# Paired butterfly outputs, quartered fifth denominator tiles and a last unit moved behind three stores, in a one-core kernel of memory attention and a spectral filter

## The chip, the core and the metric

The kernel runs on one core of a Trainium2 chip. That core has five engines that run side by side, each through its own queue in order: TensorE (PE, matrix products into PSUM; its weight loads are shown apart as PEld), VectorE (DVE), ScalarE (ACT), GpSimd (POOL) and SyncE (SP, which here issues most transfers between SBUF and DRAM). The metric is the device time of one execution in microseconds (us); less is better. Operands are fp32, or fp32 cut to a shorter mantissa (fp32r), which the kernel uses as a high and a low part.

## What is computed

Two independent parts stand beside each other in the output. Part A is an attention with a compressive memory: 2048 tokens of width 576, 32 heads of 18, four segments of 512 tokens. Part B is a global filter: a two-dimensional real FFT of a 2048 × 576 array, a product with a complex weight, and the inverse FFT.

```python
def _A_ref(x, wq, wk, wv, wo, beta):          # S=2048, H=32, Dh=18, N=4, L=512
    ...
    for s in range(N):
        qs, ks, vs = q[:, :, s], k[:, :, s], v[:, :, s]
        p = _softmax(einsum("bhqd,bhkd->bhqk", qs, ks) * scale + mask)
        a_dot = einsum("bhqk,bhkd->bhqd", p, vs)
        pq = phi(qs)
        num = einsum("bhld,bhde->bhle", pq, M)
        den = einsum("bhld,bhd->bhl", pq, z)[..., None] + 1e-6
        outs.append(g * num / den + (1.0 - g) * a_dot)
        pk = phi(ks)
        M = M + einsum("bhld,bhle->bhde", pk, vs)
        z = z + einsum("bhld->bhd", pk)
    return concat(outs) @ wo
def _B_ref(x, w_r, w_i):
    X = rfft2(x) * (w_r + 1j * w_i)
    return irfft2(X, s=(S, D))
```

## The kernel before

**Stages.** The FFT over the 2048 rows is split as 128 × 4 × 4. The forward part (`FFT.forward`, L108) does the transform over columns and the 128-point one as matmuls, in 20 iterations `u`, and leaves 16 complex blocks in the tile `Z` of 128 partitions × 4 × 4 × 2 × 290: block (b, a), real and imaginary part, 290 frequencies. Then come radix-4 butterflies over a and over b on DVE (`bf`, L199), the twiddle factors between them (`tws`, L210), the weight product and the way back (`middle`, L232; `last`, L270). `FFT.inverse` (L285) brings the blocks back with matmuls. From 72 to 280 us, between the forward and the inverse matmuls, stand the projections of part A (`projections`, L549): for each of four groups g nine q/k units and four v units. Then attention runs over 132 turns (`attention`, L941), and a tail projects the last segment (`last_proj`, L901).

**The FFT's vector work is paced.** `stage1`, `middle` and `last` are generators; each `yield` is one step. `Pace` (L88) holds them in a queue with a hand-written total: 61 steps for the four first-stage generators, 165 for the middle and 40 for the last. The forward transform takes one step per iteration for u < 14 (the first generator is queued at u = 7) and two from u = 14. The projections spread what is left, less 10 for the last butterfly (`tot=pace.left-10`, L558), over their units: `w=tot/(36+16*2.4)` steps for a q/k unit and 2.4 times as many for a v unit, 0.4 of them before and 0.6 after the second half of the unit's products. The order in which each engine sees its work in these stages is the order of the code.

**A q/k unit** (`qk_unit`, L466) makes 14 products of 512 columns (L464) into a PSUM bank, and then splits the result into three bfloat16 parts while later units run on PE: ACT copies it (L477) and, where needed, takes a negative-side exponential (L480, L481); DVE forms the feature map (L483) and subtracts the first part (L484); ACT copies the second part (L491); PE subtracts it (L493, after the first seven products of the unit after next); ACT copies the third (L494).

**A butterfly** (`bf`) has ten steps: four DVE operations over whole blocks (128x580) into temporaries, two whole ones for outputs 0 and 2, and four of half a block (128x290) for the outputs 1 and 3, whose parts are rotated by 90 degrees (L204 to L209). **A twiddle** (`tws`) multiplies a block by exp(i a): ACT makes cos(a) and sin(a) times the whole block (L218, L219), DVE combines halves (L224, L226). Where the angle is 90 degrees (exponent 4), the same work is done.

**Denominators.** For segments 1 to 3 `den` (L781) multiplies the feature maps of the queries by z. The heads lie in five tiles, four of 7 heads (126 rows) and one of 4 heads (72 rows). z stands in `zst`, zero apart from one column per head, 32 columns wide. Tiles 0 to 3 go to the four 32-row column groups of one PSUM bank; tile 4 follows one step later, alone, into a fresh PSUM tile. Each of the two is copied by ACT (L789). Five transfers then write the rows to `dD` in DRAM, and `recip` (L752) reads them back, inverts them and writes them in bfloat16 parts. `den` is one of the background generators `bg` of the attention, which `run_bg` (L953) advances by about 1.2 steps a turn; `later(1, f)` (L907) hands a transfer to the end of the next turn. `post` (L800) gives these products their PSUM bank, of which there is one.

**The tail.** Unit u of `last_proj` is one half row (288 columns) of one of four token blocks; its 15 products run over five tiles t. Before the change the order is: t = 0 to 2 for units 0 to 6, t = 3 for them, t = 0 to 3 for unit 7 (L1041), then t = 4 for all, each followed by a copy out of PSUM on ACT or DVE and, after the second half of a block, a store of 128x576 (L1048). The fifth tile's low part is made on DVE at L893.

## Time and profile before

| | us |
|---|---|
| median of 3 runs (lowest to highest) | 710.68 (708.92 to 712.03) |
| the profiled execution | 709.86 |
| its span, first to last instruction | 708.2 |
| PE busy in the span | 678.8 |
| DVE busy | 544.8 |
| ACT busy | 455.8 |
| GpSimd busy | 194.6 |

One execution is profiled in every instruction. Its span leaves out what lies before the first and after the last instruction. A row of the timeline names start, duration, engine, line, operation, written and read tiles, shape (partitions x elements), the count of equal instructions merged, and in brackets how long the engine had been idle and what released it. A row of the waits view names who waited for whom, the sum, how often, and the longest. Products overlap one another on PE, so what a product costs is the time to the start of the next one, not its own duration. "q" behind an engine's name is its queue: it marks the issue of a transfer.

### The profile page before, as it was taken

The page shows a single profiled execution, that of the slowest core. Times are in us where ns is not written, and L with a number is a line of the kernel's source. Part 1 is how long each engine was busy: PE and PEld are TensorE (multiplying, and loading weights), DVE is VectorE, ACT ScalarE, POOL GpSimd, SP SyncE. Part 2 cuts the span into 40 slices and gives each one's busy share as a digit, 9 for nine tenths or more (in the row PEclk, how much of TensorE's full clock was granted, in tenths as well). Part 3 has the DMA queues.
Part 4 walks back from the last instruction along what each step waited for, and adds up shares of the span by engine and source line. Part 5 has one row for each costly group of instructions (what it writes and reads, how often), then busy time and mean ns, then how long its engine had stood idle before and what let it go on. Part 6 is the DMA issues. An engine that isn't in the chain of part 4 may idle for free.

```text
span 708.2 us, 14408 instructions
## 1 busy us (share of the span) xinstructions
PE 678.8 (96%) x4991; PEld 501.3 (71%) x4991; DVE 544.8 (77%) x1258; ACT 455.8 (64%) x1004; POOL 194.6 (27%) x392
## 2 busy tenths in 40 slices
PE   4999999999999999999999899999999999998997
PEld 3999769879779879998954454445566445663587
DVE  4899969899699789797787787988657876567533
ACT  3777796585686484544388777777656776567421
POOL 3111000100200102665135333444233752235310
PEclk9999999999999999999999999999999999999999
DMA  9897355666384679999338976976766766442151
GB/s 328 256 305 202 115 141 187 186 185 202 100 250 156 178 196 311 202 240 267 100 114 210 190 163 143 207 182 167 154 129 181 182 166 154 92 122 65 29 164 74
DMA packets 71146, 123.80 MB, mean 175 GB/s; under 512 B 12184, under 2 KB 39174, under 8 KB 67482
## 3 DMA queue, kind: packets, MB, share of 16 engines
q1 hardware_dynamic: 64422, 106.89, 57.4%
q0 software_dynamic: 5632, 15.76, 8.2%
q8 instruction: 39, 0.64, 0.4%
q10 hardware_dynamic: 1020, 0.25, 0.2%
q14 instruction: 33, 0.27, 0.1%
HBM read 82.10 MB, written 39.81 MB: 172 GB/s over the span
## 4 chain that ended last, share of the span: by engine, by line
PE 68%; DMA 8%; ACT 4%; DVE 4%; POOL 2%; issue 2%; SPq 0%; ACTq 0%; DVEq 0%; POOLq 0%
PE pj L464 12%; PE pv L734 9%; PE s L656 9%; PE pjv L464 8%; PE po L877 6%; PE i L309 3%; PE i L298 3%; PE s L705 3%; PE s L709 2%; DMA yb<-yout 2%; PE pn L807 2%; PE s L669 2%; PE pm L532 2%; PE s L714 2%; DMA Ks<-qkD 1%
## 5 line engine op out<-in xcount | busy, mean ns | idle before, releaser
L664 DVE CUSTOM_DVE_ANT_0 junk<-s,x 128x512 bf16<-128x512 f32 x248 | 137.0, 552 | 58.0 <-PE s L656 52.6
L719 POOL TENSOR_SCALAR_AFFINE_SELECT P<-P 128x512 f32<-128x512 f32 (+2 forms) x132 | 78.5, 626 | 112.9 <-ACT P L706 104.1
L670 DVE TENSOR_REDUCE mx<-s 128x4 f32<-128x512 f32 x128 | 87.7, 685 | 5.6 <-PE s L669 3.7
L706 ACT ACTIVATE P<-s 128x512 f32<-128x512 f32 x128 | 77.7, 607 | 10.8 <-PE s L705 3.8
L734 PE MATMUL pv<-P,vs 128*32 128x512 f32 (+3 forms) x1024 | 82.5, 439 | 0.1
L715 ACT ACTIVATE P<-s 128x256 f32<-128x256 f32 x128 | 49.8, 389 | 46.1 <-PE s L714 45.7
L711 ACT ACTIVATE P<-s 128x512 f32<-128x512 f32 x128 | 77.4, 605 | 2.4 <-PE s L710 2.2
L656 PE MATMUL s<-Ks,Qs 108*128 108x384 bf16 (+3 forms) x256 | 69.1, 301 | 1.5 <-DMA ux<-uD 1.0
L734 PEld LDWEIGHTS pv<-P,vs 128*32 128x32 f32 x1024 | 26.9, 109 | 45.3 <-issue 35.1
L464 PE MATMUL pj<-x,wqkh 128*128 128x512 f32 x162 | 56.5, 409 | 0.0
L208 DVE TENSOR_TENSOR Z<-t,t 128x290 f32<-128x290 f32 (+1 forms) x96 | 48.4, 553 | 0.1
L656 PEld LDWEIGHTS <-Qs 108*128 108x128 bf16 x320 | 31.5, 98 | 23.5 <-issue 12.1
L208 DVE TENSOR_TENSOR t<-Z 128x580 f32<-128x580 f32 x64 | 46.1, 755 | 0.0
L669 PE MATMUL s<-tri,idb 128*128 128x128 bf16 x256 | 43.0, 219 | 0.0
L522 POOL MEMSET vt<- 128x32 f32 x16 | 2.3, 162 | 141.3 <-PE pm L532 119.5
L298 PE MATMUL i<-civ,Y 128*128 128x256 f32 (+1 forms) x288 | 39.3, 289 | 0.2 <-POOL Y L283 0.2
L298 PEld LDWEIGHTS i<-civ,Y 128*128 128x128 f32 (+1 forms) x288 | 36.5, 181 | 1.0 <-POOL Y L283 0.4
L309 PE MATMUL i<-itab,T 128*128 128x290 f32 (+1 forms) x224 | 36.7, 306 | 0.5 <-DVE yout L317 0.4
L464 PE MATMUL pj<-x,wqkl 128*128 128x512 f32 x90 | 35.6, 395 | 0.0
L464 PE MATMUL pj<-xh,wqkl 128*128 128x512 f32 x90 | 35.5, 395 | 0.0
L143 PE MATMUL f<-ftab,eh 128*128 128x290 f32 x128 | 25.3, 321 | 10.7 <-DMA ftab<-ftab 10.6
L464 PE MATMUL pj<-xh,wqkh 128*128 128x512 f32 x90 | 35.5, 395 | 0.0
(210 smaller groups left out, 1806.3 us busy)
## 6 DMA issues: line engine op xcount, KB each, us to landing
qkD<-sp SPq DMA_DIRECT2D x32, 384.0 KB
xin<-xb SPq DMA_DIRECT2D x16, 384.0 KB
cfw<-cfw POOLq DMA_DIRECT2D x16, 384.0 KB, 4.7
civ<-civ POOLq DMA_DIRECT2D x16, 384.0 KB, 9.0
vs<-vD SPq DMA_DIRECT2D x16, 330.0 KB
vD<-vt SPq DMA_DIRECT2D x16, 311.0 KB
W<-w SPq DMA_DIRECT2D x16, 290.0 KB
yb<-yout SPq DMA_DIRECT2D x16, 290.0 KB
```

Of the source, the lines that this page charges most:

```text
L208: v.tensor_tensor(o,a,b,op=op)
L298: nc.tensor.matmul(p[:m,k],Y[i][:,q,c*128:c*128+m],cc[:,hl,o:o+256],start=n==0,stop=n==5)
L309: nc.tensor.matmul(p,x,t,start=n==0,stop=n==6)
L464: s.nc.tensor.matmul(out,a,b,start=i==0,stop=i==len(L)-1)
L656: nc.tensor.matmul(out,Q[:108,h,128*i:128*i+128],K[:108,h,:128*(i+1)],start=True,stop=True)
L664: nc.vector.tensor_tensor_reduce(out=junk[:,:w],in0=src,in1=s.mask[:,512-w:],scale=1.0,scalar=-3.0e38, op0=OP.add,op1=OP.max,accum_out=s.m ...
L669: nc.tensor.matmul(pa[:,o+w-128:o+w],s.idb,s.tri,start=False,stop=True,skip_group_check=True)
L670: nc.vector.tensor_reduce(out=s.mx[k][:,hh],in_=pa.rearrange("p (b c) -> p b c",c=128),axis=mybir.AxisListType.X,op=OP.max)
L706: nc.scalar.activation(P[0][:,hh],p0,AF.Exp,scale=SC)
L711: nc.scalar.activation(P[1][:,hh],p1,AF.Exp,scale=SC)
L719: nc.gpsimd.affine_select(out=x[:,r],in_=x[:,r],pattern=[[0,r.stop-r.start],[1,128]],compare_op=OP.is_ge,fill=0.0,base=0,channel_multiplie ...
L734: nc.tensor.matmul(s.pvt[32*hh:32*hh+32,128*j:],vt[:,j,19*h:19*h+32],mv[0][:,hh,mv[1]],start=j==0,stop=j>1,skip_group_check=True)
```

## The change

`bf` now works on numbered slots of `Z` (a slot is 290 columns; `slots(i, j)` is a pair of them, j − i apart, which may be negative). The outputs 1 and 3 are made in pairs: one operation writes the real part of one and the imaginary part of the other over 128x580, with the two parts of the fourth temporary read in reverse order. So a butterfly has eight steps. Where output 2 would be turned by 90 degrees afterwards (`turn`), the butterfly writes its two halves turned, in nine steps, and `tws` leaves that block out. `tws` lets ACT make only the cross terms, ±sin(a) times the other half, in two operations of 128x290, and DVE does cos(a) times the block plus the cross terms in one SCALAR_TENSOR_TENSOR of 128x580, in place. The totals of `Pace` become 44, 140 and 32, and 8 steps are kept back for the last butterfly.

z of the fifth tile moves to columns 8 to 11 of its `zst` tile. In `den` its product is cut into four of 128 columns, one for each column group of the bank that holds tiles 0 to 3, accumulated onto it. One ACT copy remains; the fifth tile's rows go out in four transfers of 4 x 128, eight in all, queued one step earlier than the five before.

In the tail the products t = 0 to 3 of unit 7 come after unit 5's copy and the third store; units 6 and 7 are stored separately, 288 columns each.

```diff
@@ -177,7 +177,7 @@
         for i in range(2):
             for x in p: next(x)
         load(3)
-        s.pace=Pace(61+165+40)
+        s.pace=Pace(44+140+32)
         for u in range(20):
             p=prep(u+2) if u+2<16 else iter(())
             if 0<u<17: ev0(u-1)
@@ -196,39 +196,42 @@
             if u>13: s.pace.take(2)
         for _ in wl: pass
         for _ in xs: pass
-    def bf(s,x,y,inv):
+    def slots(s,i,j):
+
+        z=s.Z.rearrange("p b a r f -> p (b a r) f"); d=j-i
+        return z[:,i:j+1:d] if d>0 else z[:,i:j-1 if j>0 else None:d]
+    def bf(s,I,inv,turn=False):
 
         v=s.nc.vector; tp=s.tp
+        x=[s.slots(i,i+1) for i in I]; y=x[2]
         t=[tp.tile([128,2,FP],F32,name=f"t{i}",tag="t",bufs=8) for i in range(4)]
-        p,m=(y[1],y[3]) if not inv else (y[3],y[1])
-        for o,a,b,op in ((t[0],x[0],x[2],OP.add),(t[1],x[0],x[2],OP.subtract),(t[2],x[1],x[3],OP.add),(t[3],x[1],x[3],OP.subtract),
-                         (y[0],t[0],t[2],OP.add),(y[2],t[0],t[2],OP.subtract),
-                         (p[:,0],t[1][:,0],t[3][:,1],OP.add),(p[:,1],t[1][:,1],t[3][:,0],OP.subtract),
-                         (m[:,0],t[1][:,0],t[3][:,1],OP.subtract),(m[:,1],t[1][:,1],t[3][:,0],OP.add)):
+        p,m=(I[3],I[1]) if inv else (I[1],I[3])
+        L=[(t[0],x[0],x[2],OP.add),(t[1],x[0],x[2],OP.subtract),(t[2],x[1],x[3],OP.add),(t[3],x[1],x[3],OP.subtract),(x[0],t[0],t[2],OP.add)]
+        if turn:
+            g,h=(t[2],t[0]) if inv else (t[0],t[2])
+            L+=[(y[:,0],g[:,1],h[:,1],OP.subtract),(y[:,1],h[:,0],g[:,0],OP.subtract)]
+        else: L+=[(y,t[0],t[2],OP.subtract)]
+        L+=[(s.slots(p,m+1),t[1],t[3][:,::-1],OP.add),(s.slots(m,p+1),t[1],t[3][:,::-1],OP.subtract)]
+        for o,a,b,op in L:
             v.tensor_tensor(o,a,b,op=op)
             yield
     def tws(s,L,inv):
 
-        nc=s.nc; v=nc.vector; A=[]; L=[x for x in L if x[1]]
-        if not L: return
-        for i in range(len(L)+1):
-            if i<len(L):
-                y,e=L[i]; a=-2*np.pi*e/16*(-1 if inv else 1)
-                t=[s.tp.tile([128,2,FP],F32,name=f"tw{k}",tag="t",bufs=8) for k in range(2)]
-                nc.scalar.activation(t[0],y,AF.Copy,scale=float(np.cos(a)))
-                nc.scalar.activation(t[1],y,AF.Copy,scale=float(np.sin(a)))
-                A.append((y,t))
-                if i==0: yield
-            if i>0:
-                y,t=A.pop(0)
-                v.tensor_tensor(y[:,0],t[0][:,0],t[1][:,1],op=OP.subtract)
-                yield
-                v.tensor_tensor(y[:,1],t[0][:,1],t[1][:,0],op=OP.add)
-                yield
+        nc=s.nc; q=[]
+        for i,e in L+[(None,0)]:
+            if i is not None:
+                a=-2*np.pi*e/16*(-1 if inv else 1); y=s.slots(i,i+1)
+                t=s.tp.tile([128,2,FP],F32,name="tw",tag="t",bufs=8)
+                for k in range(2): nc.scalar.activation(t[:,k],y[:,1-k],AF.Copy,scale=float((-np.sin(a),np.sin(a))[k]))
+            if q:
+                z,c,x=q.pop(0)
+                nc.vector.scalar_tensor_tensor(z,z,c,x,op0=OP.mult,op1=OP.add)
+            if i is not None: q.append((y,float(np.cos(a)),t))
+            yield
     def stage1(s,b):
-        x=[s.Z[:,b,a] for a in range(4)]
-        yield from s.bf(x,x,False)
-        yield from s.tws([(x[c],b*c) for c in (2,1,3)],False)
+        I=[8*b+2*a for a in range(4)]
+        yield from s.bf(I,False,b==2)
+        if b: yield from s.tws([(I[c],b*c) for c in (2,1,3) if b*c!=4],False)
     def middle(s,wp):
         nc,io=s.nc,s.io; v=nc.vector
         Ws=[]
@@ -238,8 +241,8 @@
             Ws.append(W)
         for i in range(3): ld(i)
         for c in range(4):
-            x=[s.Z[:,b,c] for b in range(4)]
-            yield from s.bf(x,x,False)
+            I=[8*b+2*c for b in range(4)]; x=[s.slots(i,i+1) for i in I]
+            yield from s.bf(I,False)
             for d in range(4):
                 W=Ws[4*c+d]
                 t=s.tp.tile([128,2,FP],F32,name="wm",tag="t",bufs=8)
@@ -253,8 +256,8 @@
                 yield
                 v.tensor_tensor(x[d][:,1],t[:,1],t2[:,0],op=OP.add)
                 yield
-            yield from s.bf(x,x,True)
-            yield from s.tws([(x[b],b*c) for b in (2,1,3)],True)
+            yield from s.bf(I,True,c==2)
+            if c: yield from s.tws([(I[b],b*c) for b in (2,1,3) if b*c!=4],True)
     def inv_setup(s,cp):
         nc,io=s.nc,s.io
         s.cp=cp; s.civ={}
@@ -270,8 +273,7 @@
     def last(s):
 
         for b in range(4):
-            x=[s.Z[:,b,c] for c in range(4)]
-            yield from s.bf(x,x,True)
+            yield from s.bf([8*b+2*c for c in range(4)],True)
             s.done=b
     def ysplit(s,u,eng=None):
         nc=s.nc; eng=eng or nc.gpsimd; b,a=divmod(u,4); x=s.Z[:,b,a]
@@ -539,13 +541,14 @@
             m=tp.tile([126,7,19],F32,name="mm")
             nc.vector.tensor_tensor(m[:r,:w],s.pm[t//3][:r,t%3,:w],s.bm[:r,:w],op=OP.mult)
             M=s.Mst[n][:r,t,:r].rearrange("p (h c) -> p h c",c=18)
-            z=s.zst[n][:r,t,:w]
+            zc=slice(0,w) if t<4 else slice(8,12)
+            z=s.zst[n][:r,t,zc]
             if n==1:
                 nc.gpsimd.tensor_copy(M,m[:r,:w,:18])
                 nc.gpsimd.tensor_copy(z,m[:r,:w,18])
             else:
                 nc.gpsimd.tensor_tensor(M,m[:r,:w,:18],s.Mst[g][:r,t,:r].rearrange("p (h c) -> p h c",c=18),op=OP.add)
-                nc.gpsimd.tensor_tensor(z,m[:r,:w,18],s.zst[g][:r,t,:w],op=OP.add)
+                nc.gpsimd.tensor_tensor(z,m[:r,:w,18],s.zst[g][:r,t,zc],op=OP.add)
     def projections(s,xp,tp,pp,wv,pace,hook):
 
         live=[]
@@ -555,7 +558,7 @@
             for l in list(live):
                 try: next(l)
                 except StopIteration: live.remove(l)
-        tot=pace.left-10
+        tot=pace.left-8
         for g in range(4):
             if g<3: xq=[s.xprep(g+1,t,(xp,s.x0)[g%2],xp,[128,512],"xst",2) for t in range(5)]
             for i in range(13):
@@ -780,17 +783,19 @@
         s.pq[g,t]=x
     def den(s,g,lane):
         nc=s.nc; tp=s.tp
-        ds,ds2=[tp.tile([128,512],F32,name=f"ds{i}",tag="ux",bufs=3) for i in range(2)]; ds2=ds2[:32]
-        for T,d in ((range(4),ds),((4,),ds2)):
-            pd=s.post("pd")
-            for t in T:
-                r=126 if t<4 else 72
-                nc.tensor.matmul(pd[32*(t%4):32*(t%4)+32],s.zst[g][:r,t],s.pq[g,t][:r],start=True,stop=True,skip_group_check=True)
-            nc.scalar.copy(d,pd[:d.shape[0]])
-            yield
-        for t in range(5):
-            w=7 if t<4 else 4
-            s.later(1,lambda t=t,w=w: nc.sync.dma_start(s.dD[g][7*t:7*t+w],ds[32*t:32*t+w] if t<4 else ds2[:w]))
+        ds=tp.tile([128,512],F32,name="ds",tag="ux",bufs=3)
+        pd=s.post("pd")
+        for t in range(4): nc.tensor.matmul(pd[32*t:32*t+32],s.zst[g][:126,t],s.pq[g,t][:126],start=True,stop=False,skip_group_check=True)
+        for j in range(4):
+            c=slice(128*j,128*j+128)
+            nc.tensor.matmul(pd[32*j:32*j+32,c],s.zst[g][:72,4],s.pq[g,4][:72,c],start=False,stop=True,skip_group_check=True)
+        nc.scalar.copy(ds,pd)
+        yield
+        for t in range(4):
+            s.later(1,lambda t=t: nc.sync.dma_start(s.dD[g][7*t:7*t+7],ds[32*t:32*t+7]))
+        for j in range(4):
+            s.later(1,lambda c=slice(128*j,128*j+128),j=j: nc.sync.dma_start(s.dD[g][28:32,c],ds[32*j+8:32*j+12,c]))
+        yield
         def chain():
             yield
             yield
@@ -1038,14 +1043,15 @@
                 if t==2 and u in (1,4): s.last_tile(3 if u==1 else 4,"rd")
         s.last_low()
         for u in range(7): s.last_proj(u,3)
-        for t in range(4): s.last_proj(7,t)
         o=[s.tp.tile([128,4,512],F32,name=f"P{i}").rearrange("p a b -> p (a b)") for i in range(2)]
         o=[o[tb//3][:,576*(tb%3):576*(tb%3)+576] for tb in range(4)]
         nc=s.nc
         for u in range(8):
-            tb,hf=divmod(u,2); s.last_proj(u,4)
+            if u==6:
+                for t in range(4): s.last_proj(7,t)
+            tb,hf=divmod(u,2); s.last_proj(u,4); c=slice(288*hf,288*hf+288) if u>5 else slice(0,576)
             (nc.vector.tensor_copy if hf else nc.scalar.copy)(o[tb][:,288*hf:288*hf+288],s.acc[u])
-            if hf: nc.sync.dma_start(s.io["ya"][1536+128*tb:1664+128*tb],o[tb])
+            if hf or u>5: nc.sync.dma_start(s.io["ya"][1536+128*tb:1664+128*tb,c],o[tb][:,c])
 
 def prio(tc,gen,off):
 
```

## The prediction

> **What bounds the kernel now.** I read the page first, then the busy time by stage, then what TensorE (PE) waits for, then the timeline at each of those waits.
>
> ```profile
> span 708.2 us, 14408 instructions
> PE 678.8 (96%) x4991; PEld 501.3 (71%) x4991; DVE 544.8 (77%) x1258; ACT 455.8 (64%) x1004; POOL 194.6 (27%) x392
> ```
>
> PE is busy for 96% of the span, so an edit is worth what it takes from PE's own work or from PE's waits. The execution took 709.86, which is 1.66 more than its span; the median of the runs, 710.68, lies 0.82 above it. The mean of the three runs and this execution is 710.4, and I use that as the base.
>
> ```profile
> 40.00:60.00 20.00, 19.88 (x140) 18.75 (x139) 19.92 (x32) 14.82 (x27) 3.34 (x7) 1.00 0.85 258
> ...
> 85.00:195.00 110.00, 107.64 (x621) 91.47 (x620) 92.89 (x176) 76.25 (x148) 7.46 (x36) 1.00 0.57 169
> 195.00:283.00 88.00, 87.99 (x517) 75.70 (x516) 77.82 (x145) 57.86 (x116) 7.28 (x29) 1.00 0.73 219
> 692.00:708.20 16.20, 11.91 (x84) 11.02 (x82) 5.88 (x10) 2.84 (x6) 0.00 (x0) 0.95 0.19 74
> ```
>
> After stretch and length, the columns are the busy us (and instructions) of PE, of weight loads, of VectorE (DVE), ScalarE (ACT) and GpSimd, then PE's granted clock, the DMA share and GB/s. The first row is a piece of the forward transform, where DVE has no idle time; the next two are the projections at full clock, with the FFT's vector work paced beside the matmuls; the last is the tail. PE lacks 2.4 us in the second row and nothing in the third. The waits of PE from 85 to 283 have a single row:
>
> ```profile
> PE pj L493 <- ACT sp L491: 2.2, 3, 1.0
> ```
>
> Three waits, 2.2 us together: all that a lighter FFT can return there.
>
> **Part 1: butterflies and twiddles.** The first rows price two-input DVE work from start to start, three wide ones and four narrow ones in a row; the other two compare operations of 512 elements.
>
> ```profile
> 106.20 2.10 DVE L208 TENSOR_TENSOR t<-Z 128x580 f32<-128x580 f32 x3
> 110.76 1.56 DVE L208 TENSOR_TENSOR Z<-t,t 128x290 f32<-128x290 f32 x4
> ...
> L484 DVE TENSOR_TENSOR pj<-pj,sp 128x512 f32<-128x512 f32 x36 | 24.9, 690 | 1.0 <-ACT sp L477 0.9
> L483 DVE SCALAR_TENSOR_TENSOR ex<-pj,ex 128x512 f32<-128x512 f32 x26 | 17.9, 689 | 17.1 <-ACT ex L481 16.9
> ```
>
> A wide operation costs 0.70 us, a narrow one 0.39. Each of 16 butterflies trades four narrow ones (1.56) for two wide ones (1.40): 2.6 saved, less 0.2 for the two turned outputs, each two narrow for one wide. Of 18 twiddles two go into those turns; 36 narrow operations (14.0) become 16 of SCALAR_TENSOR_TENSOR (11.2 if it runs as TENSOR_TENSOR does, 689 against 690 ns above). No row shows outputs with two strides or a reversed input; their ends are 0.70 and the 0.78 of the pair replaced, and I take 0.70. DVE thus saves about 5 us in all, beside matmuls and worth nothing by itself. Where DVE is full (first row above), seven single steps are taken; only the seventh turns from narrow to wide, +0.31, and behind it (u=14 on) no more input has to be prepared. I cost it at nothing; with that cover gone it is 0.3.
>
> ACT gains more. A twiddle now costs two activations of 580 elements, 0.59 apart; then two of 290. The nearest row of that width is the pair at L525:
>
> ```profile
> 88.59 0.43 ACT L408 CAST wvh<-raw 128x288 fp32r<-128x288 f32 x1 [0.53 <-DMA raw<-wv]
> ...
> 91.91 0.69 ACT L218 ACTIVATE tw<-Z 128x580 f32<-128x580 f32 x1
> 92.50 0.68 ACT L219 ACTIVATE tw<-Z 128x580 f32<-128x580 f32 x1
> 93.08 0.42 ACT L408 CAST wvh<-raw 128x288 fp32r<-128x288 f32 x1
> ...
> 93.92 0.58 ACT L491 CAST sp<-pj 128x512 bf16<-128x512 f32 x1
> 94.55 0.38 PE L493 MATMUL pj<-sp,nid 128*128 128x512 bf16 x1 [0.70 <-ACT sp L491]
> ...
> 99.74 0.38 PE L493 MATMUL pj<-sp,nid 128*128 128x512 bf16 x1 [0.97 <-ACT sp L491]
> ...
> 112.31 0.71 ACT L525 COPY vt<-pjv 128x288 f32<-128x288 f32 x2
> ```
>
> So 1.17 becomes 0.71 per twiddle, 18 × 1.17 = 21 becomes 16 × 0.71 = 11: ACT saves 10. The first wait reads off these rows: L491 of unit 4 stands behind a twiddle, and without its 1.17 it would have ended 0.5 before PE wanted it. Where twiddles fall is arithmetic. The FFT has 266 steps (61+165+40), then 216 (44+140+32). The forward transform takes 19, the inverse gets the last butterfly's 10, then 8; the rest is spread over 74.4 weights: 3.19 steps per q/k unit before, 2.54 after. Before, the forward transform stops 9 steps into the second butterfly of the first stage; 1+7 finish it, 10 are the third butterfly's own, so its twiddles begin after 18 steps, 18/3.19 = 5.6 units in, and stretch into unit 6. After, 1 step finishes the second, 9 are the third's (it is the turned one), 10/2.54 = 3.9: they begin in unit 4 and are over at unit 5's start. Hence no ACT step stands in front of L491 of units 4 and 5, and the waits of 0.70 and 0.97 go. In unit 4 itself ACT idles 0.53 in front of a load (first row), which covers most of a new pair there. The third wait is DVE's:
>
> ```profile
> 189.44 0.76 DVE L208 TENSOR_TENSOR Z<-t,t 128x580 f32<-128x580 f32 x1
> 190.12 0.68 DVE L483 SCALAR_TENSOR_TENSOR ex<-pj,ex 128x512 f32<-128x512 f32 x1
> 190.72 0.68 DVE L484 TENSOR_TENSOR pj<-pj,sp 128x512 f32<-128x512 f32 x1
> 192.08 0.38 PE L493 MATMUL pj<-sp,nid 128*128 128x512 bf16 x1 [0.56 <-ACT sp L491]
> ```
>
> Two wide steps stand there ahead of L483 and L484 (one shown). Unit 2 of group 2 begins 2 × 18.6 + 2 = 39.2 weights in, at step 19 + 125 = 144 of 266 before, the fourth of a butterfly, and at step 19 + 99.6 = 118.6 of 216 after, the seventh: one wide step in front of L483 instead of two, 0.70 less, and the 0.56 goes. What is late next is unit 8: its L484 will follow three twiddle operations in unit 9, which wait for ACT. I charge 0.2 and take **−2.0**, ends −2.2 and, if each wait only moves, 0.
>
> **Part 2: denominators, three times.** Products on four column groups run side by side; a lone one has PE to itself.
>
> ```profile
> 423.24 1.28 PE L734 MATMUL pv<-P,vs 128*32 128x512 f32 x16
> 424.46 0.28 PE L656 MATMUL s<-Ks,Qs 108*128 108x256 bf16 x1
> ...
> 510.05 1.04 PE L788 MATMUL pd<-pq,zst 126*32 126x512 f32 x8
> 511.03 0.28 PE L656 MATMUL s<-Ks,Qs 108*128 108x256 bf16 x1
> ...
> 512.41 1.04 PE L788 MATMUL pd<-pq,zst 72*32 72x512 f32 x2
> 513.39 0.28 PE L656 MATMUL s<-Ks,Qs 108*128 108x256 bf16 x1
> ```
>
> Four tiles take 0.98 to the next product's start, the fifth alone another 0.98. The new form, four products of 512 columns and four of 128 on the same groups, has the shape of a pv burst: 1.22. Bounds for the quarters: nothing, and 0.98 for a lone product; I take 0.24, since the pv row has the same shape. 1.96−1.22 = 0.74, three times **−2.2**, ends 0 and −2.9. One copy on ACT goes too, hidden beside matmuls. The other columns of the fifth tile's sums are the same GpSimd operation of the same size, and the ring of ux buffers gets one user fewer: nothing.
>
> The Trainium skill ("TensorE: Matmul & The Clock Gate", Back-to-back issue gap) gives 518 cycles at 2.4 GHz for 512 columns, 0.43 us for the two instructions of the lone product. By that the part would be about 0.3 a time, an estimate; the 0.98 of the trace disagrees. "FP8 and Floating Point Precision" of the skill (TensorE Precision Notes) has true fp32 in four passes, by the same estimate 0.86, which the trace bears out.
>
> SP issues eight transfers instead of five, one loop turn earlier.
>
> ```profile
> 432.74 1.64 SPq L793 DMA_DIRECT2D dD<-ds  x5
> 438.54 0.32 SPq L638 DMA_DIRECT2D Qs<-qkD  x1
> SPq L745 <- ACT P L706: 8.6, 1, 8.6
> SPq L638 <- PE s L669: 1.3, 1, 1.3
> 448.99 0.32 PE L656 MATMUL s<-Ks,Qs 108*128 108x384 bf16 x1 [1.03 <-DMA ux<-uD]
> ```
>
> At 0.33 each that is 2.6 us, and it falls into the 8.6 that SP stands in front of L745. Without this cover the stack loads behind would be 1.0 later. The load at 438.54 waits for PE's L669, so it moves up with PE, and the wait at 448.99 stays near 1.03 instead of swallowing the gain.
>
> **Part 3: tail.**
>
> ```profile
> 696.80 7.61 PE po L906 x55
> 698.80 0.69 DVE L893 TENSOR_TENSOR P<-ux,P 72x512 fp32r<-72x512 f32 x1 [0.74 <-ACT P L889]
> 701.16 0.29 PE L906 MATMUL po<-wol,P 72*128 72x288 f32 x1
> 702.61 2.75 SPq L1048 DMA_DIRECT2D ya<-P  x4
> DMA  0000000079989999999995899940000000000000
> ```
>
> PE's last 55 products (0.138 each) stay as many and end at the same point; unit 7's twelve move behind three stores. In the last row (702 to 709 in slices of 0.175) the four stores fill 19 slices, 3.3 us, 0.83 each. With half as much in the last one: **−0.4**, ends 0 and −0.8. The wait this could add: the t=4 products begin 12 × 0.138 = 1.66 earlier, at 699.4, and the third needs the low part that L893 ends at 699.49; it is wanted at 699.64, a margin of 0.15. Past that PE stands and u=7's copy and store behind it, at most 0.4, the gain of this part.
>
> Sum: −2.0−2.2−0.4 = −4.6: 705.3 against this execution's 709.86, **705.8** on the base of 710.4.
>
> **Rivals.**
> - The projection waits move instead of going: −2.6, 707.8. For it: unit 8. Against it: the count leaves at most one wide step before L484 in nearly every q/k unit.
> - Attention is pinned by transfers: the time from the denominators comes back as waits like that of 448.99. −2.4, 708.0. Against it: only one PE wait there is a DMA's.
> - Slower: the new twiddle operation waits on DVE for ACT halves that queue behind L477, L480 and L481, and L483/L484 of the projection stand behind it. From L477 to L491 six operations of about 0.57 (L483, L484 and L491 above) follow one another, 3.4 us; 21 products of the next units give, by the row below, 21 × 0.233 = 4.9. So it decides from 1.5 us of twiddle time in between. Two pairs cost 1.4. Four groups of twiddles at 1.4: +5.6−2.6, 713.4. For it: DVE and ACT now alternate more tightly. Against it: the operations lag their activations by one step.
> - The lone product really occupies PE only as two instructions of a projection, 2 × 0.233 = 0.47, and the rest of its 0.98 is a pause that stays: part 2 is 3 × (0.47−0.24) = −0.7, 707.3. That is what the rule on the gap would make of it.
> - The edit does not do what it says: the quarters run one after the other, 0.98 again, part 2 gives nothing: 708.0.
>
> ```profile
> 100.55 3.27 PE pj L464 x14
> ```
>
> **Numbers.** Chances: forecast 0.58 (own range 704 to 707.5), moved waits 0.16, pinned 0.08, slower 0.12, pause 0.03, serial quarters 0.03. Range 703.8 to 709.5: it holds all but the slower case and the outer edges. Half a per cent, 3.6 us, is about what a measurement here tells from no change. Faster by more (under 707.1): 0.52 of the forecast, 0.03+0.02+0.01 of others, 0.58; slower 0.11; same 0.31.
>
> **What would show it.** Part 1: the row of PE waits for L491 falls from 2.2 towards 0.2. Part 2: L788 with 16 instructions in about 1.22, one copy, no second burst. Part 3: the last row of stores ends 0.4 earlier after the last DVE copy, and L906 shows no wait for L893. I am wrong if new waits at L493 stand in units 5 to 9 or if waits for Qs or Ks grow after 440.

## The result and the profile after

The changed kernel took **701.49 us** (median of 6 runs, 700.99 to 702.32) against 710.39 (6 runs, 707.33 to 712.03) of the kernel before: ratio 0.9889, 95% interval 0.9866 to 0.9913. A second set of runs, told below, gave 702.98 (6 runs, 701.52 to 705.14) against 709.22: ratio 0.992, interval 0.9902 to 0.9939. The sign was forecast rightly. The size was not: 4.6 us were forecast, the two ratios give 7.9 and 5.7, and both medians lie below the range's lower end of 703.8. The profiled execution after the change took 701.35, before it 709.86.

Lines after the change are a few higher: L491 and L493 are now L493 and L495, L656 is L659, L705 and L706 are L708 and L709, L788 with its second form is L788 and L791, L886 is L891, L893 is L898, L906 is L911, L1047 and L1048 are L1053 and L1054.

The first part of the page after the change:

```profile
span 699.6 us, 14387 instructions
...
PE 674.5 (96%) x5009; PEld 500.8 (72%) x5009; DVE 539.0 (77%) x1208; ACT 444.9 (64%) x997; POOL 193.6 (28%) x392
```

DVE lost 5.8 us and ACT 10.9; forecast were 5 and 10. PE has 18 more products and as many more weight loads than before. Both numbers matter later. By stretches (same columns as before, ends moved with the stages):

```profile
85.00:192.00 107.00, 106.58 (x618) 90.87 (x617) 89.74 (x152) 71.20 (x147) 6.92 (x36) 1.00 0.59 174
192.00:280.00 88.00, 88.00 (x520) 75.94 (x519) 73.59 (x123) 54.88 (x115) 7.56 (x29) 1.00 0.74 217
```

In the first row PE lacks 0.42 where it lacked 2.36. Here are ACT and PE where the first wait of 0.70 was, then two rows of PE's waits: the one behind the denominators, where the prediction read 1.03, and what is left in the projections:

```profile
91.64 0.43 ACT L410 CAST wvh<-raw 128x288 fp32r<-128x288 f32 x1
91.97 0.62 ACT L437 CAST xh<-xst 128x512 fp32r<-128x512 f32 x1
92.50 0.58 ACT L493 CAST sp<-pj 128x512 bf16<-128x512 f32 x1
...
93.38 0.39 PE L495 MATMUL pj<-sp,nid 128*128 128x512 bf16 x1
```

```profile
PE s L659 <- DVE mx L673: 1.2, 2, 1.0
...
PE pj L495 <- ACT sp L493: 0.4, 1, 0.4
```

No twiddle stands ahead of the L493 at 92.50 any more, and the product at 93.38 has no bracket: PE didn't stand. The one wait that is left is unit 8's; it was 0.14 before and is 0.42 now. The denominators and the end:

```profile
503.82 1.29 PE L737 MATMUL pv<-P,vs 128*32 128x512 f32 x16
504.92 1.04 PE L788 MATMUL pd<-pq,zst 126*32 126x512 f32 x8
505.78 0.40 PE L791 MATMUL pd<-pq,zst 72*32 72x128 f32 x8
506.12 0.28 PE L659 MATMUL s<-Ks,Qs 108*128 108x256 bf16 x1
```

```profile
690.77 0.69 DVE L898 TENSOR_TENSOR P<-ux,P 72x512 fp32r<-72x512 f32 x1 [0.74 <-ACT P L894]
...
691.66 0.43 PE L911 MATMUL po<-woh,P 72*128 72x288 f32 x2
...
696.45 0.46 DVE L1053 COPY P<-po 128x288 f32<-128x288 f32 x1 [2.00 <-PE po L911]
```

The burst takes 504.92 to 506.12, 1.20 us. The low part that L898 makes ends at 691.46, and the products that use it follow without a bracket. The last DVE copy starts 3.2 before the end of the span; before, the same copy (704.50 in a span of 708.2) started 3.65 before it.

How far PE's products of the changed kernel lie ahead of the same products before, by the starts in the two traces (worked out from the traces, not a view of the page):

```
stretch                                    gained there, us
up to 85                                   0.3
projections, to 283                        3.0   (0.85 + 1.12 + 0.72 + 0.36 + 0.17 + 0.04 - 0.29)
inverse transform, 283 to 355              0.8   (0.6 of it at the wait for yout)
attention outside the next two rows        0.0   (up to 0.6 either way at single places)
three bursts of denominators               2.3   (0.73 + 0.84 + 0.75)
near 680, product for rr                   0.9
688 to 694, output ring and rd             0.7
last product to the end of the span        0.5
```

A burst's row goes from its first product to one after both its groups, some 60 products on; all eight kernels with quarters beside the other tiles give 0.73 to 0.84 for each burst this way. The three forecast parts are there with 3.0, 2.3 and 0.5, which is 5.8. The other rows, 2.7 us together, were not forecast. Of before's waits these belong to them: the first to the product near 680, which needs rr (the reciprocals of the denominators), the second to the inverse transform, where PE needs a free output buffer (yout), the third to the row 688 to 694:

```profile
PE pb L886 <- DVE ux L887: 0.8, 1, 0.8
...
PE i L309 <- DVE yout L317: 0.4, 1, 0.4
...
PE pb L886 <- DMA rd<-rrD: 0.3, 1, 0.3
```

The third wait is there in this one profile alone: the other 16 have 0.1 of idle time there at most, also those of kernels with before's code at that place. So the 0.5 gained at it can't be credited to the change.

**Theory 1**: the parts are independent and were mis-sized. **Theory 2**: the excess is scatter of the transfers. **Theory 3**: the parts act on each other, or on something else in the kernel, through SP's queue or the transfers. The experiments follow. Each ratio is against the kernel before, run beside it, and a gain given with a ratio is that ratio's part of 710.

### The profile page after: what moved, and what is told of

Read it like the earlier page. It is cut to its first block, busy times and chain, and to the rows that moved or that the text cites. A ratio compares the mean times of both kernels' runs of the same rounds, so it can differ in the third digit from the quotient of the medians.

```text
span 699.6 us, 14387 instructions
## 1 busy us (share of the span) xinstructions
PE 674.5 (96%) x5009; PEld 500.8 (72%) x5009; DVE 539.0 (77%) x1208; ACT 444.9 (64%) x997; POOL 193.6 (28%) x392
## 4 chain that ended last, share of the span: by engine, by line
PE 79%; DVE 6%; ACT 5%; DMA 4%; issue 3%; POOL 3%; SPq 0%; ACTq 0%; DVEq 0%; POOLq 0%
PE pj L466 15%; PE s L659 9%; PE pv L737 9%; PE pjv L466 8%; PE po L882 6%; PE i L300 4%; PE i L311 4%; PE s L708 3%; PE f L143 3%; PE s L712 2%; PE c L163 2%; PE po L911 2%; PE pm L534 2%; PE s L672 2%; PE pn L812 2%
## 5 line engine op out<-in xcount | busy, mean ns | idle before, releaser
L673 DVE TENSOR_REDUCE mx<-s 128x4 f32<-128x512 f32 x128 | 87.7, 685 | 5.2 <-PE s L672 3.3
L709 ACT ACTIVATE P<-s 128x512 f32<-128x512 f32 x128 | 77.8, 608 | 10.4 <-PE s L708 3.1
L659 PE MATMUL s<-Ks,Qs 108*128 108x384 bf16 (+3 forms) x256 | 69.2, 301 | 1.9 <-DVE mx L673 1.2
L216 DVE TENSOR_TENSOR Z<-t,t 128x580 f32<-128x580 f32 (+1 forms) x66 | 46.5, 738 | 0.1
L659 PEld LDWEIGHTS <-Qs 108*128 108x128 bf16 x320 | 31.5, 98 | 19.9 <-issue 9.5
L485 DVE SCALAR_TENSOR_TENSOR ex<-pj,ex 128x512 f32<-128x512 f32 (+1 forms) x28 | 19.3, 688 | 22.6 <-ACT ex L483 22.5
```

The lines of the kernel that those rows point to most:

```text
L216: v.tensor_tensor(o,a,b,op=op)
L659: nc.tensor.matmul(out,Q[:108,h,128*i:128*i+128],K[:108,h,:128*(i+1)],start=True,stop=True)
L673: nc.vector.tensor_reduce(out=s.mx[k][:,hh],in_=pa.rearrange("p (b c) -> p b c",c=128),axis=mybir.AxisListType.X,op=OP.max)
L709: nc.scalar.activation(P[0][:,hh],p0,AF.Exp,scale=SC)
```

## Experiments: one part at a time

**The FFT part alone**

With slots, bf, tws, stage1, middle and last as in the diff of the change:

```
-        s.pace=Pace(61+165+40)
+        s.pace=Pace(44+140+32)
...
-        tot=pace.left-10
+        tot=pace.left-8
```

> Before with the butterflies, the twiddles and their step counts alone. Theory 1 (the parts are independent and mis-sized: the projections' waits cost more than their idle rows, and the lighter inverse stage adds about 1): projections -2.8, inverse transform -1.0, start -0.3 at most, together 4 us faster, ratio 0.994 to 0.995; the waits L493 <- L491 gone, one of 0.4 left in unit 8, the wait L309 <- L317 of 0.4 gone. Theory 2 (forecast's size right, the rest of the gain is scatter of the transfers in the kernel before): 2.0 us faster, ratio 0.997. Theory 3 (the lighter vector work also brings the reciprocals' transfers of the tail forward): more than 5 us, and the tail's wait L886 <- L887 of 0.77 gone.

706.97 against 710.35, ratio 0.996 (0.9941 to 0.9978), 2.8 us: between the 4 of theory 1 and the 2.0 of theory 2. The waits of L493 went as expected. But PE's waits in this kernel's profile have two rows that neither kernel's own profile has in this size:

```profile
PE pb L856 <- DMA rr<-rrD: 1.8, 1, 1.8
...
PE i L311 <- DVE yout L319: 1.3, 1, 1.3
```

The products are 2.3 us ahead at 405 and 0.8 behind the kernel before at 466: the gain of the projections was lost in front of the load of rr. The wait alone doesn't explain it. PE's clock fell behind the gap (the number before the last two):

```profile
460.00:463.00 3.00, 1.17 (x16) 0.60 (x9) 0.67 (x3) 0.19 (x1) 1.58 (x3) 1.00 0.87 142
...
464.00:465.00 1.00, 1.00 (x5) 0.56 (x4) 1.00 (x2) 0.49 (x1) 0.21 (x1) 0.50 0.35 57
465.00:466.00 1.00, 1.00 (x8) 0.71 (x7) 1.00 (x4) 0.98 (x3) 0.00 (x0) 0.50 1.18 397
```

The gap was 1.83 us long, and the products behind it, at half the clock, lost another 1.3 against the kernel before.

**The denominators alone**

With den as in the diff of the change:

```
-            z=s.zst[n][:r,t,:w]
+            zc=slice(0,w) if t<4 else slice(8,12)
+            z=s.zst[n][:r,t,zc]
```

> Before with the denominators alone (quarters, one copy, eight transfers a turn earlier). Theory 1: three times 0.74 to 0.85, 2.2 to 2.6 us faster, ratio 0.9965, each burst 1.22 and no second one. Theory 3b (the earlier transfers also take waits of the stack loads and of the tail away): 3.5 to 4.5 us faster, and the wait L656 <- DMA ux of 1.03 at 449 gone. Serial quarters or pinned attention: under 0.5 us.

705.94, ratio 0.9945 (0.9925 to 0.9966), 3.9 us. In the trace the three bursts give 0.73, 0.84 and 0.77, together 2.3, and near 680 another 0.9 is gained. The profiled execution (708.63) is the slowest of the seven: near 337 it stands 1.72 us for yout, and there too the clock falls, to 0.50 between 339 and 342:

```profile
340.00:342.00 2.00, 2.00 (x10) 1.77 (x10) 1.07 (x4) 0.77 (x2) 0.00 (x0) 0.50 0.17 63
```

The wait near 449 didn't go: it is the 1.0 under the name L671 here and under L673 in the changed kernel. From start to start that step is 1.30 in 14 of the 17 profiles, whether the view names the stack load, the load of x or DVE's mx as its releaser (1.01 to 1.21 in the other three). So I read it as DVE's, as a transfer's would differ from run to run; no run tests this.

**The tail alone**

```
-        for t in range(4): s.last_proj(7,t)
...
         for u in range(8):
+            if u==6:
+                for t in range(4): s.last_proj(7,t)
...
-            if hf: nc.sync.dma_start(s.io["ya"][1536+128*tb:1664+128*tb],o[tb])
+            if hf or u>5: nc.sync.dma_start(s.io["ya"][1536+128*tb:1664+128*tb,c],o[tb][:,c])
```

> Before with the tail alone (unit 7's products behind three stores, last store in halves). Theory 1: 0.4 to 0.6 us faster, ratio 0.9993, the end of PE to the end of the span 0.55 shorter and nothing else changed. Theory 3c (the new order itself shortens the wait for rd and rr, 1.6 us between 668 and 704 in the two traces): 1.6 to 2.1 us faster. Rival: a wait of up to 0.4 for L893's successor takes the gain: same time.

710.08, ratio 1.0003 (0.9985 to 1.0021). The time can't resolve a term of half a microsecond. The trace can: the last DVE copy starts at 703.59 in a span of 706.8, 3.2 before the end instead of 3.65. No wait for L893 was added. The tail's order itself took nothing from the wait near 680 (1.0 idle here), so theory 3c fell.

**Butterflies alone**

Against the FFT part alone, with tws as it was before (two activations of 580, two narrow operations), and the same in stage1:

```
-        s.pace=Pace(44+140+32)
+        s.pace=Pace(53+149+32)
...
-            yield from s.bf(I,True,c==2)
-            if c: yield from s.tws([(I[b],b*c) for b in (2,1,3) if b*c!=4],True)
+            yield from s.bf(I,True)
+            yield from s.tws([(s.slots(I[b],I[b]+1),b*c) for b in (2,1,3)],True)
```

> Before with the butterflies' rotated outputs in pairs alone: twiddles as before, no turned outputs, 53+149+32 steps. Theory 1 reads the FFT's gain as ACT's twiddle pairs out of L491's way in units 4 and 5 and one wide DVE step out of L484's way in unit 41: here the twiddles keep their two wide activations, only their place moves, so the waits at L493 move rather than go: projections 0 to -1.5, inverse -0.5 to -1, together 1 to 2 us faster (ratio 0.998). Rival (the gain is VectorE's relief, not ScalarE's): 3 us or more faster here, ratio under 0.996.

714.89, ratio 1.0076 (1.0051 to 1.0102): **5.4 us slower**, which neither theory expected. ACT in front of unit 4's cast (here L498), the products of PE there, and two stretches:

```profile
92.48 0.69 ACT L226 ACTIVATE tw<-Z 128x580 f32<-128x580 f32 x1
93.07 0.67 ACT L227 ACTIVATE tw<-Z 128x580 f32<-128x580 f32 x1
93.77 0.59 ACT L501 CAST sp<-pj 128x512 bf16<-128x512 f32 x1
94.25 0.69 ACT L226 ACTIVATE tw<-Z 128x580 f32<-128x580 f32 x1
94.84 0.68 ACT L227 ACTIVATE tw<-Z 128x580 f32<-128x580 f32 x1
...
96.26 0.58 ACT L498 CAST sp<-pj 128x512 bf16<-128x512 f32 x1
```

```profile
94.10 0.40 PE L471 MATMUL pj<-x,wqkh 128*128 128x512 f32 x1
96.89 0.59 PE L500 MATMUL pj<-sp,nid 128*128 128x512 bf16 x1 [2.40 <-ACT sp L498]
```

```profile
94.50:96.90 2.40, 0.01 (x1) 0.00 (x0) 0.96 (x2) 2.40 (x6) 0.00 (x0) 0.97 0.68 209
96.90:103.40 6.50, 6.50 (x18) 4.71 (x18) 3.46 (x8) 4.63 (x9) 0.00 (x0) 0.50 0.58 118
```

With fewer steps in a butterfly the twiddles come earlier, and two of the old wide pairs, 2.4 us of ACT, now stand in front of unit 4's cast. PE stands 2.40 us. Then the granted clock (the column before the last two) is 0.50 over 6.5 us. The 18 products from 96.89 to the next start at 103.67 take 6.78 us; the same 18 took 3.82 in the kernel before (94.55 to 98.37, clock 1.00). So the stall cost about 2.4 and the slow clock another 3.0. The Trainium skill ("TensorE: Matmul & The Clock Gate", Part 1) has the clock fall to half after at least one idle window of about 3.4 us. The gap here was 2.40, and 1.83 and 1.72 in the two kernels above, so the measurement decides: gaps shorter than that were enough. Further on, three of the old wide pairs (ACT from 112.88 to 116.36) stand in front of the same cast, and PE stands 1.47 at 117.98. This kernel also stands 2.48 us at the start of the inverse transform, in a gap that the profile puts down to nothing ("issue"):

```profile
288.45 3.48 DVE L216 TENSOR_TENSOR Z<-t,t 128x580 f32<-128x580 f32 x3
291.86 0.68 DVE L337 TENSOR_TENSOR T<-i,T 128x512 fp32r<-128x512 f32 x1
292.64 2.36 PE L305 MATMUL i<-civ,Y 128*128 128x256 f32 x18 [2.48 <-issue]
```

By the order of times PE waited there for L337, which reads its results out of PSUM and ended 0.1 before PE went on. DVE came to it late, behind six butterfly steps in a row, of which the last two took 1.76 and 1.13 instead of 0.76 while GpSimd ran L290. No run tests this reading.

**Twiddles alone**

Against before, with the new tws and the old bf, and the same in stage1:

```
-        s.pace=Pace(61+165+40)
+        s.pace=Pace(52+156+40)
...
-            yield from s.tws([(x[b],b*c) for b in (2,1,3)],True)
+            if c: yield from s.tws([(8*b+2*c,b*c) for b in (2,1,3)],True)
```

> Before with the new twiddles alone (half activations, one SCALAR_TENSOR_TENSOR), butterflies as before, no turned outputs, 52+156+40 steps. Theory A (what counts is which ScalarE work stands ahead of L491 at units 4, 5 and 41: a pair of 0.71 instead of 1.17): with 52 steps the first twiddles fall into units 5 and 6; each takes 0.46 less from ScalarE, so the waits of L493 fall from 2.2 to about 1, and no stall is long enough to cost TensorE its clock, as the 2.4 us stall with butterflies alone did: 1.5 to 3 us faster, ratio 0.996 to 0.998. Theory B (only both halves together place the steps rightly): no gain or slower, ratio over 1.000.

707.78 against 710.16, ratio 0.9962 (0.9942 to 0.9981), 2.7 us. From its timeline and its waits:

```profile
91.05 1.46 ACT L221 ACTIVATE tw<-Z 128x290 f32<-128x290 f32 x4
92.41 0.42 ACT L407 CAST wvh<-raw 128x288 fp32r<-128x288 f32 x1
92.73 0.62 ACT L434 CAST xh<-xst 128x512 fp32r<-128x512 f32 x1
93.25 0.57 ACT L490 CAST sp<-pj 128x512 bf16<-128x512 f32 x1
```

```profile
PE pb L853 <- DMA rr<-rrD: 1.3, 1, 1.3
...
PE pj L492 <- ACT sp L490: 0.4, 1, 0.4
```

Two whole pairs stand at the same place as in the kernel with butterflies alone, but take 1.36 to the next start instead of 2.4, and PE doesn't stand: all three waits went. So the twiddles' shorter ACT time is enough for part 1 by itself. The waits also show the one for rr again.

## Experiments: what holds the rest

**The changed kernel without the tail**

Against the changed kernel:

```
+        for t in range(4): s.last_proj(7,t)
...
-            if u==6:
-                for t in range(4): s.last_proj(7,t)
...
-            if hf or u>5: nc.sync.dma_start(s.io["ya"][1536+128*tb:1664+128*tb,c],o[tb][:,c])
+            if hf: nc.sync.dma_start(s.io["ya"][1536+128*tb:1664+128*tb],o[tb])
```

> The changed kernel with the tail as it was. The parts alone gave -3.4 (FFT), -4.4 (denominators) and -0.3 (tail). Theory A (the parts add, the tail is worth 0.3 to 0.6): 7.8 us faster, about 702.3, ratio 0.989. Theory B (the reordered tail is worth 1.5 us once the stages ahead of it are lighter, as the trace comparison of the tail reads): 703 to 704, ratio 0.991.

704.36 (700.95 to 707.11), ratio 0.9907 (0.9873 to 0.9941). Six us of scatter; the tail's share isn't resolved, and both theories lie inside.

**Denominators with late transfers, and early transfers alone**

Against the denominators alone (e6), and against before (e7):

```
         nc.scalar.copy(ds,pd)
         yield
+        yield
         for t in range(4):
...
-        yield
         def chain():
```

```
             nc.scalar.copy(d,pd[:d.shape[0]])
-            yield
-        for t in range(5):
-            w=7 if t<4 else 4
-            s.later(1,lambda t=t,w=w: nc.sync.dma_start(s.dD[g][7*t:7*t+w],ds[32*t:32*t+w] if t<4 else ds2[:w]))
+            if T!=(4,): yield
+            for t in T:
+                w=7 if t<4 else 4
+                s.later(1,lambda t=t,w=w: nc.sync.dma_start(s.dD[g][7*t:7*t+w],ds[32*t:32*t+w] if t<4 else ds2[:w]))
+        yield
```

> Before with the denominators' quarters and one copy, but all eight transfers one turn later, where the five of the kernel before stood. Theory A (the second half of the 4.4 us of the denominators' part comes from SP's transfers that move into its wait in front of L745, so that the stack loads and the reciprocals behind them go out earlier): only TensorE's 3 x 0.8 is left, or less because eight transfers stand there instead of five: 1.4 to 2.4 us faster, ratio 0.9965 to 0.998. Theory B (the gain is TensorE's and the ring's alone): 4.4 us faster as with early transfers, ratio 0.994.

> Before with the denominators' products and two copies as they were, and only the five transfers one turn earlier. Theory A: 2 us faster, ratio 0.997, the waits of L656 for stack loads (1.03 at 449) gone or smaller. Theory B: no difference, ratio 0.999 to 1.001.

e6: 706.80, ratio 0.995 (0.9928 to 0.9971). e7: 709.17, ratio 0.9978 (0.9957 to 1.0). The quarters with late transfers gave 3.6 where 1.4 to 2.4 were expected of theory A: that speaks against the transfers as the main source of the denominators' gain, though the interval (2.1 to 5.1) reaches that range. Early transfers alone gave 1.6, barely told from nothing. In e6's profile the product for rr near 463 stands 1.0 (its row: "PE pb L857 <- DMA rr<-rrD"); in e7's it doesn't stand.

**Instructions of PE, without packing**

Against before, the lone product as four of 128 columns, on the same column group and in its own bank as before:

```
-                nc.tensor.matmul(pd[32*(t%4):32*(t%4)+32],s.zst[g][:r,t],s.pq[g,t][:r],start=True,stop=True,skip_group_check=True)
+                for c in ((slice(0,512),) if t<4 else [slice(128*j,128*j+128) for j in range(4)]):
+                    nc.tensor.matmul(pd[32*(t%4):32*(t%4)+32,c],s.zst[g][:r,t],s.pq[g,t][:r,c],start=True,stop=True,skip_group_check=True)
```

> Before with only the fifth tile's lone product cut into four products of 128 columns, one after the other, in its own bank as before: as many TensorE instructions as in the changed kernel (36 more with their weight loads) but no packing. Theory A (the 0.8 to 1.3 us of L886 near 680 come from a 16 KB load of TensorE's instructions that falls on the write of rrD; it comes every 256 instructions, so 36 more of them ahead of it move it off): rrD to rr in 1.9 to 2.1 instead of 3.0 to 3.5 us, the wait of L886 gone, products as long as before (0.98 to 1.1 for the four): 0.5 to 1.2 us faster, ratio 0.9985 to 0.9995. Theory B (the shorter path there comes from the earlier or fewer transfers): rrD to rr 3.0 or more, same time or slower.

708.70 against 709.22, ratio 0.9993 (0.9978 to 1.0007): consistent with half a microsecond, not resolved. Its profile settles two things. First the price of a lone product: four quarters in series take 0.97 to the next start, like the one of 512 columns.

```profile
430.52 1.04 PE L789 MATMUL pd<-pq,zst 72*32 72x128 f32 x8
431.49 0.28 PE L656 MATMUL s<-Ks,Qs 108*128 108x256 bf16 x1
```

Second, the wait near 680. SP writes the reciprocals (rrD) and then waits until they have landed to load them as rr. Before, and in this kernel:

```profile
669.35 0.39 SPq L768 DMA_DIRECT2D rrD<-rw  x1
672.48 0.32 SPq L772 DMA_DIRECT2D rr<-rrD  x1
```

```profile
671.08 0.39 SPq L768 DMA_DIRECT2D rrD<-rw  x1
672.96 0.33 SPq L772 DMA_DIRECT2D rr<-rrD  x1
```

3.13 us and 1.88. What lies between is in the records of single packets. Queue q8 of before's page carries instructions:

```profile
q8 instruction: 39, 0.64, 0.4%
```

That is 39 packets of 16 KB. PE's 4991 products and 4991 weight loads over 39 are 256 instructions a packet; it is PE's code. Each takes 0.9 to 2.1 us. The Trainium skill ("Advanced Engine Details and Errata", ISA Cache) has a line of 16 KB hold 256 instructions, and the numbers agree. Over all kernels profiled here (packet's start against the issue of the write, its length, the issue of the load, and how much longer the product near 680 took to start than it should):

```
kernel           PE products  packet at   long  rr loaded  product near 680
before           4991         +0.69       1.27  3.12       +0.93
FFT alone        4991         +0.70       1.13  3.01       +1.30
tail alone       4991         +0.74       1.16  3.04       +1.21
butterflies      4991         +0.67       1.04  2.81       +0.42
early transfers  4991         +1.13       0.88  3.26        0.00
twiddles         4991         +1.35       0.94  3.48       +0.55
before, 4 yout   4991         +0.67       0.97  2.81       +1.18
FFT + early      4991         +0.74       1.22  3.20       +0.22
changed          5009         -0.43       0.88  1.85        0.00
denominators     5009         -0.53       0.99  1.87       +0.06
without tail     5009         -0.50       1.21  1.89        0.00
den., late       5009         -0.41       1.39  2.14        0.00
changed again    5009         -0.61       1.24  1.87        0.00
changed, 4 yout  5009         -0.23       0.89  1.89        0.00
split, unpacked  5009         -0.55       0.96  1.88       +0.16
changed, late    5009         -0.38       1.03  1.86        0.00
old butterflies  5009         -0.55       1.17  1.86        0.00
```

With 4991 products the packet falls onto the write. Before, 360 packets of 256 bytes start between 670.3 and 670.8 and the other 24 between 671.3 and 671.9. 24 of 384 are a sixteenth, the share of one of the 16 DMA engines: the one that loads code, by this reading, comes out last. With 5009 the load of the code comes about half a microsecond ahead of the write's issue, and is over, or nearly, when the write's packets begin (0.9 behind the issue). The kernel of this experiment ("split, unpacked") has nothing of the change but the number of instructions, and it behaves like the changed one, with 0.16 left of 0.93. So this 0.9 us needs neither the denominators' packing nor their transfers: where code is loaded is enough, by 0.8 of it. That the late write always costs PE its wait isn't so: two kernels with early transfers and the old number (early transfers, FFT + early) have the late write and hardly a wait. In the changed kernel both hold, and either would have done.

**The changed kernel again, and a fourth yout buffer in both**

```
-            o=yl.tile([128,2,FP],F32,name="yout",bufs=3)
+            o=yl.tile([128,2,FP],F32,name="yout",bufs=4)
```

> The changed kernel once more, beside the others on one chip, since its six runs lie within 1.3 us while those of the partial kernels scatter by 4 to 6. Theory A (the parts add to 7.8 us, and the six runs were on the lucky side of a scatter that the transfers make): median 702 to 703, spread 4 us or more. Theory B (all parts together leave TensorE no wait for a transfer, so nothing is left that scatters): median 701.0 to 702.0, spread under 2 us.

> The changed kernel with four instead of three buffers for yout. Profiles so far show TensorE's L309 (or its successor) waiting 0 to 1.9 us near 335 for a yout buffer whose store is late. Theory A (that ring is a source of the scatter in every variant): no such wait, 0.5 to 1 us faster than the changed kernel beside it and less spread. Theory B (the DMA queues are full there and the wait only moves to the next stage): same time as the changed kernel.

> Before with four instead of three buffers for yout. Theory A: the wait of L309 for L317 (0.4 to 1.7 us in the profiles of kernels without other change there) goes, 0.6 to 1.5 us faster, ratio 0.998 to 0.999. Theory B: the time comes back at the stack loads near 397 and 448, ratio 0.9995 to 1.0005.

Again: 702.98 (701.52 to 705.14), ratio 0.992 (0.9902 to 0.9939), with a spread of 3.6: nearer to theory A. With four buffers 702.55, ratio 0.9907 (0.9893 to 0.9922). Before with four buffers 709.10, ratio 0.9998 (0.9984 to 1.0012). The wait for yout is absent from both profiles with four buffers, and the times are those with three: theory B, though the intervals don't exclude half a microsecond. That wait comes and goes in kernels whose code up to there is the same: the changed kernel has none in two profiles, while without the tail it is 1.1 and with late transfers 1.2. With the old butterflies, below, it is 1.8:

```profile
PE i L307 <- DVE yout L315: 1.8, 1, 1.8
```

So the 0.6 at that wait, most of the inverse transform's row in the comparison above, can't be credited to the change.

**Late transfers in the changed kernel, the changed kernel with old butterflies, and early transfers with the FFT part**

e13 is the changed kernel with the edit of e6. e15 is the FFT part alone with the edit of e7. e14 is the changed kernel with the old bf:

```
-        s.pace=Pace(44+140+32)
+        s.pace=Pace(52+156+40)
...
-            yield from s.bf(I,True,c==2)
-            if c: yield from s.tws([(I[b],b*c) for b in (2,1,3) if b*c!=4],True)
+            yield from s.bf(x,x,True)
+            if c: yield from s.tws([(I[b],b*c) for b in (2,1,3)],True)
...
-        tot=pace.left-8
+        tot=pace.left-10
```

> The changed kernel with its eight transfers of the denominators one turn later, where the five of the kernel before stood. Theory A (with TensorE earlier by the FFT part, the load of rr near 463 becomes late unless the denominators' transfers leave earlier: the FFT alone and the twiddles alone showed waits of 1.8 and 1.3 us for rr there, the changed kernel none): a wait of 1 to 2.2 us of the low-rank product for rr near 458, 1.5 us slower than the changed kernel, 703.5 to 705, ratio 0.993 to 0.995. Theory B (those waits were chance): no wait for rr, 702 to 703, ratio 0.990 to 0.992.

> The changed kernel with the old butterflies: new twiddles, denominators and tail alone, 52+156+40 steps. The twiddles alone took all three waits of L493 away in the profile. Theory A (the butterflies' pairs are worth nothing by themselves, as VectorE's time lies beside the matmuls): same time as the changed kernel, 702 to 703, ratio 0.990 to 0.992. Theory B (lighter VectorE work is worth 1 us where VectorE is full, before 60 and near 397): 1 us slower than the changed kernel, 703.5 to 704.5.

> Before with the FFT part and, of the denominators' part, only the five transfers one turn earlier; products and copies as before. Theory A: no wait for rr near 460, so the FFT part gives its whole 3.5 to 4.5 us and the early transfers no more than that: 705.5 to 706.5, ratio 0.9935 to 0.995, against 0.996 for the FFT alone; the wait of the tail for rr near 680 (the instruction load, no instructions added) stays. Theory B: the wait for rr near 460 stays, 0.996.

e13: 704.81 against 709.84, ratio 0.9915 (0.9887 to 0.9942). e14: 702.43, ratio 0.9879 (0.9855 to 0.9904). e15: 707.07, ratio 0.9953 (0.9927 to 0.9978). In e13's profile the wait for rr is back:

```profile
PE pb L859 <- DMA rr<-rrD: 0.7, 1, 0.7
```

Over the 17 profiles, the product for rr near 460 stands (1.1 to 2.2 from start to start instead of 0.31) in four: FFT alone, twiddles alone, denominators with late transfers, changed with late transfers. All four have late transfers; three have PE ahead of the kernel before, the fourth (e6) has eight late transfers instead of five. No kernel with early transfers has the wait, nor has one with five late transfers and PE not ahead. But before with four yout buffers has five late transfers and PE 2.1 ahead there, and no wait, so the two together do not suffice. In the four kernels the load of rr takes 7.2 to 8.2 us from its issue to its landing, in the other thirteen 4.5 to 6.0; what lengthens it stays open. What the wait is worth in time is not shown either: e13's median lies 2.4 above e14's, run beside it, but the intervals overlap, and e15's 0.9953 isn't told from the FFT part's 0.996.

e14 is as fast as the changed kernel: the butterflies' pairs, alone a loss, add nothing that can be told from nothing to the twiddles. No kernel tried is told from the changed one as faster.

## Why the prediction was wrong in size

**What bounds the kernel** was right: PE, by its own work and its waits.

**Part 1, the step "three waits, 2.2 us together: all that a lighter FFT can return there"**, was wrong. The waits view gives a product's idle time, which begins where the one before it is modelled to end. From start to start, the steps into L493 at the three places took 1.10, 1.37 and 0.95 where an undisturbed one takes 0.24: 0.86, 1.13 and 0.72 more, 2.70 together against 2.23 of idle time. Four more places show next to no idle time, so the view doesn't list them: 0.12 each at 195.68, 199.29 and 202.90, and 0.17 at 256.07. Here is the first of them before, the step from 195.32 to 195.68:

```profile
195.32 0.40 PE L464 MATMUL pj<-x,wqkh 128*128 128x512 f32 x1
195.68 0.38 PE L493 MATMUL pj<-sp,nid 128*128 128x512 bf16 x1
```

All four went with the change. With the 0.29 that unit 8 took back (0.2 was charged) the part gave 3.0, not 2.0. Which twiddles stand where was right for the changed kernel; the shorter pair on ACT would have been enough, as the twiddles alone showed. The values per operation were right. From the groups of the changed kernel:

```profile
L216 DVE TENSOR_TENSOR Z<-t,t 128x580 f32<-128x580 f32 x62 | 44.8, 756 | 0.1
...
L228 DVE SCALAR_TENSOR_TENSOR Z<-Z,tw 128x580 f32<-128x580 f32 x16 | 11.7, 757 | 4.8 <-ACT tw L225 4.8
...
L225 ACT ACTIVATE tw<-Z 128x290 f32<-128x290 f32 x32 | 12.2, 440 | 2.6 <-DVE Z L216 2.5
```

Outputs with two strides and reversed inputs cost what plain wide ones do (756), and SCALAR_TENSOR_TENSOR as much (757). The DVE time saved was worth nothing by itself, as forecast: e14 gives no sign of it, within its interval.

**Part 2** was right in its mechanism and its row: 1.20 measured, 1.22 forecast. By starts the three bursts gave 0.73, 0.84 and 0.75, 2.3 against 2.2 forecast, and the denominators alone 2.3 too. The size was right as well. The rivals of a pause (0.23 a burst) and of serial quarters (nothing) fell.

**Part 2, the step that SP's eight transfers, "one loop turn earlier", cost and bring nothing**, was half right. They cost nothing that shows. But the wait for rr near 460 came in four profiles with late transfers and in none with early ones, so the pinned rival had its place, another one than I named, and the early transfers that belong to the change may be its remedy. The wait near 449 stayed at its length, as forecast; that a transfer releases it was probably misread.

**Part 3** was right: 0.4 forecast, 0.5 measured in the trace (0.4 with the tail alone), no wait for L893 added.

**The step that failed for the rest is the sum itself**: it has no term outside the three edits. The 0.9 near 680 comes from PE's number of instructions, which moved a load of code off a small write. The range was built from the three parts and their rivals alone. With this term and part 1 at its measured size the sum would have stood at the range's lower end.

Sum of what is shown: 3.0 + 2.3 + 0.5 + 0.9 = 6.7. Means over all runs are 702.3 (12 runs of the changed kernel) and 710.2 (95 of the one before), 7.9 apart. The last 1.2 stays open: the start, the yout wait and the wait for rd near 693 differ by as much between kernels with the same code at these places, and what such a wait costs differs too (below). The changed kernel's two profiles have no gap over 1.1 us behind the start.

The slower rival didn't happen in the changed kernel, yet the butterflies alone came close to it: 2.4 us of twiddles between L477 and L491, past the 1.5 from which it was to decide, are the largest single piece of the 5.4 that this kernel lost. There the pairs on ACT themselves stood in front of the cast, not a DVE operation that waits for them, and the rival had no term for the clock.

## What to carry to other kernels

Measure a wait from start to start against an undisturbed step, and take the idle time only as a lower bound. A paced helper stream is a matter of place as much as of cost: the butterflies alone lost 5.4 us, most of it by moving long twiddles in front of a cast, and the twiddles alone gained 2.7 by being short at that same place. Where small transfers that something waits for are near the end, expect half a microsecond to a whole one from changes that only alter the number of instructions, and put it into the range.

## What the runs showed of the hardware

Whether a gap costs TensorE its clock is not settled by its length alone. In the 17 profiles, all of its gaps behind 90 us that lasted up to 1.6 us were followed by a clock of 1.00. Of six between 1.7 and 2.5, three were followed by 0.50 (1.72 near 337 in the denominators alone, 1.83 near 462 in the FFT alone, 2.40 near 97 in butterflies alone; the half clock lasted 3.4 us in the first two and 6.8 in the third) and three by 1.00 (1.75 and 1.97 near 333 in e14 and e15, 2.48 near 292 in butterflies alone). So a wait of about 1.8 us cost its own length or over 3. That may be part of why the times of one kernel scatter by 4 us and more; no run here showed it.

PE's code arrives in packets of 16 KB, one for every 256 instructions, each of 0.9 to 2.1 us; a small write under one was ready 2.8 to 3.5 us after its issue, one that came just behind it 1.9 to 2.1. Fp32 products of 128 columns take a quarter of one of 512 in series (0.97 for four), and on four column groups four of them take 0.34 to the next product's start.
